# Cluster numbers through DRAM: broadcast by transfers and compared on VectorE, in place of one-hot rows transposed on TensorE

## The chip, the cores and the metric

The kernel runs on one core of one Trainium2 chip. Its five engines each have an instruction stream of their own: TensorE (PE, with its weight loads PEld), VectorE (DVE), ScalarE (ACT), GpSimd (POOL) and SyncE (SP), which here issues nearly all DMAs. They meet only at semaphores. TensorE writes to PSUM, eight banks of 2 KB a partition; the other operands lie in SBUF. The metric is the device time of one execution in microseconds (us), the median of several runs. All times below come from the runs, the profile's page or the trace.

## What is computed

The reference is a clustered attention, followed by a mixing stage that the change does not touch.

```python
q_n = q / (norm(q) + 1e-06); k_n = k / (norm(k) + 1e-06); c_n = centroids / (norm(centroids) + 1e-06)
q_assign = np.argmax(np.einsum('bhsd,hcd->bhsc', q_n, c_n), axis=-1)
k_assign = np.argmax(np.einsum('bhsd,hcd->bhsc', k_n, c_n), axis=-1)
mask = q_assign[:, :, :, None] == k_assign[:, :, None, :]
scores = scale * np.matmul(q, k.transpose(0, 1, 3, 2))
scores = np.where(mask, scores, -1000000000.0)
attn = softmax(scores)              # shifted by the row's largest score
x = np.matmul(attn, v)              # then: theta = x @ w_theta, rotation, token mixing, channel layer
```

There are 4 batches, 8 heads, 768 positions, 64 numbers a head and 16 clusters. Every query and every key belongs to the cluster whose centroid fits it best, and a query sees only the keys of its own cluster.

## The kernel before

**Pairs and units.** Two heads fill the 128 partitions, 64 each, so there are 16 pairs (`pi`, 0 to 15). The attention of a pair is cut into 12 units: for each half of the queries (`a`, 384 positions) the six blocks of 128 keys. Units are numbered through, 12 to a pair, and the loop `while u < NUT + LAG or todo` writes the work of one unit after another. `in_order` (L440) ties the instructions of each engine, SP included, into exactly that order. Work that is not needed in every unit is entered in a list `todo` by `at_unit` and `stages`, and is written at the end of its unit, behind what every unit has.

What a unit holds, in its order:

- `scores(u)` (L335): eight matmuls (four products for each head), then the exponentials on ScalarE (L344) and a running sum on GpSimd (L350). The products are q's and k's high and low parts, and one product of the masks `mk` and `mq`.
- in odd units `row_max(u + 11)` (L304): eight matmuls of the product and the mask for 128 queries of the unit eleven ahead, then two reductions on VectorE (L319), which give the largest score of each query. The matmuls write to two tiles of two banks each, which the next row maxima take again.
- in even units `weighted` (L387) twice: eight matmuls of exponentials and v (`av`).
- the entries of `todo`.

The mask is a matmul as well. `mq` has, for each head, 16 rows with a one in the row of the query's cluster, and `mk` has -2^60 in the rows of all clusters but the key's own. Row 32 of each half of `mq` gets the query's largest score with the sign turned, brought there by `shift_row` (L323): TensorE transposes the maxima (`mt`), ScalarE copies them (`mr`), and two DMAs write them to the row. So the product adds the mask and the shift to the scores.

**The cluster numbers** are made by the generator `assign(pi)` (L217), one stage per `yield`, entered for pair `pi` by `prepare` (L457) at the units of `A_UNITS`, counted from the start of the pair two before:

1. unit -2: two loads of the raw q and k (`raw`).
2. unit 1: logits of q and k against the centroids (`lg`, eight matmuls), copied to SBUF by ScalarE (`lgs`).
3. unit 3: three transposes (`lt`), so that the positions lie on partitions; VectorE finds the largest logit of each (`mx`) and marks where it is reached (`eq`, L246).
4. unit 4: the marks times the numbers 16 to 1 (L250), and the largest of these is the cluster's number (`rr`, L252).
5. unit 6: `ohp` (L254), a one in the place of the number, by comparing it with all 16.
6. units 9 and 11: six transposes each on TensorE (`ot`, L262) turn the ones of q and of k back, and ScalarE copies them to `mq` (L264) and, scaled and shifted, to `mk` (L266).

Pair 0 goes through all of it at the start, before any unit, and pair 1 in the eleven units with negative numbers, which hold row maxima but no scores.

**Around it.** `part_hi` (ScalarE) and `part_lo` (GpSimd) split q and k into high and low parts, at `HI_UNITS` and `LO_UNITS`. `sums(pi)` (L352) adds up the rows of exponentials on TensorE (`sm`), copies them by ScalarE (`se`), writes them to DRAM, reads them in another layout, takes the reciprocal on VectorE (L378), writes that to DRAM and reads it broadcast over 64 partitions (`rb`), at the units of `SUMS` of the next pair. `normalise` multiplies on GpSimd and writes the result to DRAM, at `NORM`. `early_weights` loads and splits the weights of the later stage, a chunk every 13 units; each chunk costs VectorE two operations four units after its start (L128, L130) and two more eight units after it (L133, L135).

**PSUM.** Scores take two banks of the pool `ps`, which has three (`bank`), and each small piece, `lg`, `lt`, `ot`, `mt` and `sm`, takes one. The banks go round in the order of the program, and a bank is written again only when its last reader is done.

Of the kernel before, what the change touches and what calls it, by code (L numbers as in the profile page):

```python
# [9 lines left out]
F32 = mybir.dt.float32  # L10
F32R = mybir.dt.float32r
BF16 = mybir.dt.bfloat16
I32 = mybir.dt.int32
AF = mybir.ActivationFunctionType
ALU = mybir.AluOpType
# [3 lines left out]
BIG = float(2.0 ** 60)  # L19
N_M = 2  # L20
N_AV = 1
LEAD = 11
PW = 256
TAIL = 2
WARM = 2
SUMS = (5, 6, 8, 10, 12)
NORM = (14, 16)
TERMS = 3
EARLY = 3
LAG = 3  # L30
# [11 lines left out]
def kernel(  # L42
# [19 lines left out]
    nc = tc.nc  # L62
    B, H, D, S = qT.shape
    P = 128
    NP = H // 2
    NT = S // P
    C = cent.shape[0] // H
# [5 lines left out]
    cpool = ctx.enter_context(tc.tile_pool(name="cpool", bufs=1))  # L73
    dram = ctx.enter_context(tc.tile_pool(name="dram", bufs=1, space=bass.MemoryType.DRAM))
# [3 lines left out]
    identf = cpool.tile([P, P], F32, name="identf")  # L78
    make_identity(nc, identf)
    identb = cpool.tile([P, P], BF16, name="identb")  # L80
# [13 lines left out]
    mbi = cpool.tile([P, 1], F32, name="mbi")  # L94
    nc.vector.memset(mbi, 0.0)
    for r in (0, 64):
        nc.vector.memset(mbi[r:r + C], -BIG)
        nc.vector.memset(mbi[r + 32:r + 33], 1.0)

    ecol = cpool.tile([P, 32], F32, name="ecol")  # L100
    nc.vector.memset(ecol, 0.0)
# [65 lines left out]
    pe = actx.enter_context(tc.tile_pool(name="pe", bufs=1))  # L167
    NPAIR = B * NP
    tsets = {}
    for x in range(3):  # L170
        x = (NPAIR + x) % 3
# [7 lines left out]
    def bank(name, pool=None):  # L179
        return (pool or ps).tile([P, 512], F32, tag="bank", name=name)  # L180
# [30 lines left out]

    NG = HS // C

    ohp = pe.tile([P, NG, 64], BF16, name="ohp")
    nc.vector.memset(ohp, 0.0)
    wb = wc.unsqueeze(1).broadcast_to([P, NG, C])
    def assign(pi):  # L217

        b, p = divmod(pi, NP)
        raws = []
        for n, src, eng in (("q", qT, nc.sync), ("k", kT, nc.scalar if pi == 0 else nc.sync)):
            raw = pw.tile([P, S], F32, tag="raw", name=f"raw{n}{pi}", bufs=3)
            st.setdefault(pi, dict(tsets[pi % 3]))["raw" + n] = raw
            eng.dma_start(out=raw, in_=src[b, 2 * p:2 * p + 2].rearrange("h d s -> (h d) s"))
            raws.append(raw)
        yield
        lg = bank(f"lg{pi}")[:, 0:HS]
        for g in range(4):  # L230
            a, n = divmod(g, 2)
            nc.tensor.matmul(  # L232
                lg[32 * g:32 * g + 32], lhsT=cb[:, p, :, :],
                rhs=raws[n][:, a * HS:(a + 1) * HS], start=True, stop=True)
        lgs = pe.tile([P, HS], F32, tag="lgs", name=f"lgs{pi}")
        nc.scalar.copy(out=lgs, in_=lg)
        yield
        lt = bank(f"lt{pi}")[:, 0:HS]
        for t in range(HS // P):
            sl = slice(t * P, (t + 1) * P)  # L240
            nc.tensor.transpose(out=lt[:, sl], in_=lgs[:, sl], identity=identf)
        ltv = lt.rearrange("p (g c) -> p g c", c=C)
        mx = pe.tile([P, NG], F32, tag="mxl", name=f"mxl{pi}")
        nc.vector.tensor_reduce(out=mx, in_=ltv, op=ALU.max, axis=AX.X)
        eq = pe.tile([P, NG, C], BF16, tag="eq", name=f"eq{pi}")
        nc.vector.tensor_tensor(  # L246
            out=eq, in0=ltv, in1=mx.unsqueeze(2).broadcast_to([P, NG, C]), op=ALU.is_equal)
        yield

        nc.vector.tensor_tensor(out=eq, in0=eq, in1=wb, op=ALU.mult)  # L250
        rr = pe.tile([P, NG], BF16, tag="rr", name=f"rr{pi}")
        nc.vector.tensor_reduce(out=rr, in_=eq, op=ALU.max, axis=AX.X)  # L252
        yield
        nc.vector.tensor_tensor(  # L254
            out=ohp[:, :, 0:C], in0=wb, in1=rr.unsqueeze(2).broadcast_to([P, NG, C]), op=ALU.is_equal)
        ohv = ohp.rearrange("p (x n j) c -> p x n (j c)", n=2, j=2)
        for n, x in enumerate(("mq", "mk")):
            yield
            ot = bank(f"ot{pi}{n}").bitcast(BF16)[:, 0:S]
            for t in range(NT):  # L260
                a, y = divmod(t, NH)
                nc.tensor.transpose(out=ot[:, t * P:(t + 1) * P], in_=ohv[:, 2 * y + a, n], identity=identb)  # L262
            if n == 0:
                nc.scalar.copy(out=st[pi][x], in_=ot)  # L264
            else:
                nc.scalar.activation(out=st[pi][x], in_=ot, func=AF.Identity, scale=BIG, bias=mbi)  # L266


    st = {}
# [19 lines left out]
    NH = NT // 2  # L289
# [111 lines left out]
    def normalise(pi):  # L401
        b, p = divmod(pi, NP)
        s = st.pop(pi)

        (nc.gpsimd if pi < NPAIR - 2 else nc.vector).tensor_tensor(
            out=s["xt"], in0=s["xt"], in1=s["rb"], op=ALU.mult)
        yield
        nc.sync.dma_start(out=xT_d[b][:, p], in_=s["xt"].rearrange("p a s -> p (a s)"))

    def early_weights():  # L410
        for c in range(NCT):
            yield from split_w(*w_th[c], w_theta[c * P:(c + 1) * P], DM, raw_pair, nc.gpsimd, CKE)
        for t in range(EARLY):
            for w, src in ((w_r, wrT), (w_i, wiT)):
                yield from split_w(*w[t], src[t * P:(t + 1) * P], S, raw_pair, nc.gpsimd, CKE)
        for c in range(NCT):
            yield from split_w(*w_c[c], w_ch[c * P:(c + 1) * P], DM, raw_pair, nc.gpsimd, CKE)
# [8 lines left out]
    def at_unit(u, fn, *a):  # L426
        todo.setdefault(u, []).append((fn, a))

    def stages(units, gen):

        for u in units:
            at_unit(u, lambda: next(gen, None))
        at_unit(units[-1] + 1, run, gen)
# [15 lines left out]
                tail[ins.engine] = ins.name  # L449


    A_UNITS = (-2, 1, 3, 4, 6, 9, 11)
    HI_UNITS = dict(q=0, k=2)
    LO_UNITS = dict(q=2, k=4)
    W_UNITS = (4, 8, 11)
    W_EVERY = 13
    def prepare(pi, gen):  # L457
        u = NU * (pi - 2)
        stages([u + k for k in A_UNITS[1 if pi == 1 else 0:]], gen)
        for n in "qk":  # L460
            at_unit(u + HI_UNITS[n], part_hi, pi, n)
            at_unit(u + LO_UNITS[n], part_lo, pi, n, nc.gpsimd)


    start = len(nc.cur_bb.bb.instructions)
    g0, g1 = assign(0), assign(1)
    next(g0)
    next(g1)
# [8 lines left out]
    for pi in range(NPAIR):  # L477
        u = NU * pi
        if pi > 0:
            prepare(pi, g1 if pi == 1 else assign(pi))  # L480
            at_unit(u - NU + 7, load_v, pi)
        for a in range(2):
            at_unit(u + a * NT - LEAD + NT, shift_row, pi, a)
        stages([u + NU + k for k in SUMS], sums(pi))
        stages([u + NU + k for k in NORM], normalise(pi))
    for x, gen in enumerate(early_weights()):
        u = W_EVERY * x
# [4 lines left out]
    u = -LEAD  # L492
# [225 lines left out]
    u = None  # L718
    for part in range(S // PW):
# [4 lines left out]
        u = add_y(B - 1, part * PW, (part + 1) * PW)  # L724
# [53 lines left out]
```

## Time and profile before

| | us |
|---|---|
| median of 3 runs | 863.45 |
| lowest and highest run | 861.3 and 863.47 |
| the profiled execution | 864.6 |
| its span on the core | 862.8 |
| granted clock of TensorE, mean | 0.982 of full speed |

| part of the span | us | TensorE busy |
|---|---|---|
| start, to the first row sums | 0 to 79 | partly, at a lower clock at first |
| pairs 1 to 14, from row sums to row sums | 80.67 to 458.64 | 369.11 of 377.97 |
| last pairs and the change to the mixing stage | 459 to 557 | with gaps |
| mixing stage | 557 to 863 | nearly all |

Over the span TensorE is busy 824.7 us, VectorE 466.8, ScalarE 402.5 and GpSimd 470.6. The rows of the profile that carry the argument are in the prediction. In rows of the chain of waits stand start, length, engine, tile and line; in rows of groups the mean of one instruction in ns stands behind the bar; in rows of the timeline the idle time ahead of an instruction and what ended it stand in brackets.

### The profile page before, as it was taken

Reading aid. Unit: us, or ns where it says so; the run is one execution under the profiler, and the core shown is the slowest. Engines: PE = TensorE matmul, PEld = TensorE weight load, DVE = VectorE, ACT = ScalarE, POOL = GpSimd, SP = SyncE. Lnnn points to the kernel's source line nnn. Section 1 sums busy time; section 2 is a strip of 40 time slices with the busy share of each in tenths; the row PEclk is TensorE's granted clock in tenths of the full one; section 3 lists DMA queues with packets and bytes.
Section 4 is the critical chain, followed back from the end, with each engine's and each line's share of the span. In section 5 each row is a group of like instructions: output and inputs, shape, how many; then the busy total and the mean of one; then the engine's idle time right before and its main releaser. Section 6 shows DMA issues by size and latency. Waiting matters only on the chain.

```text
span 862.8 us, 14648 instructions
## 1 busy us (share of the span) xinstructions
PE 824.7 (96%) x5863; PEld 599.2 (69%) x5863; DVE 466.8 (54%) x642; ACT 402.5 (47%) x802; POOL 470.6 (55%) x295
## 2 busy tenths in 40 slices
PE   5899899999999999999999989799999999999998
PEld 2655566565656555555666458589888988899998
DVE  4576576665775686477665188744423442343222
ACT  3246555565656555545655556432333333333220
POOL 3067668767887687677776636735122512251231
PEclk9699999999999999999999999899999999999999
DMA  2211222323223322213331152201200120010001
GB/s 94 65 53 45 88 86 65 128 87 101 80 88 111 112 76 93 81 53 102 99 119 57 56 178 98 73 1 50 98 2 1 50 98 1 1 49 26 1 13 63
DMA packets 27190, 59.09 MB, mean 68 GB/s; under 512 B 7793, under 2 KB 12657, under 8 KB 26737
## 3 DMA queue, kind: packets, MB, share of 16 engines
q1 hardware_dynamic: 26976, 57.75, 21.0%
q8 instruction: 46, 0.75, 0.4%
q10 hardware_dynamic: 144, 0.39, 0.1%
q14 instruction: 24, 0.19, 0.1%
HBM read 45.25 MB, written 12.78 MB: 67 GB/s over the span
## 4 chain that ended last, share of the span: by engine, by line
PE 77%; DVE 14%; DMA 4%; issue 2%; ACT 2%; POOL 1%; SPq 0%; ACTq 0%; DVEq 0%; POOLq 0%
PE y L648 21%; PE sc L300 16%; PE av L393 12%; PE m L300 7%; PE tp L581 6%; PE cy L671 4%; DVE nm L319 4%; PE cp L671 2%; DMA rawq<-in_qT_dram 2%; PE lg L232 2%; PE sm L360 2%; PE ot L262 1%; DVE w L130 1%; DVE w L135 1%; DVE eq L250 1%
## 5 line engine op out<-in xcount | busy, mean ns | idle before, releaser
L319 DVE TENSOR_REDUCE nm<-m 128x1 f32<-128x768 f32 x192 | 174.6, 950 | 145.5 <-PE m L300 145.5
L344 ACT ACTIVATE at<-sc 128x384 f32<-128x384 f32 x384 | 167.3, 489 | 122.8 <-PE sc L300 118.1
L350 POOL TENSOR_TENSOR acc<-at,at 128x768 f32<-128x768 f32 x64 | 120.7, 1886 | 99.7 <-ACT at L344 99.6
L393 PE MATMUL av<-at,vt 128*64 128x384 f32 x768 | 145.8, 501 | 0.0
L350 POOL TENSOR_TENSOR acc<-acc,at 128x768 f32<-128x768 f32 x64 | 123.1, 1923 | 28.9 <-ACT at L344 27.7
L602 POOL TENSOR_TENSOR zlc<-ab,zhc 128x512 fp32r<-128x512 f32 x24 | 31.9, 1330 | 170.8 <-ACT zhc L600 169.5
L300 PEld LDWEIGHTS sc<-hq,hk 64*128 64x128 f32 x384 | 41.4, 185 | 88.1 <-ACT at L344 60.9
L300 PE MATMUL sc<-hq,hk 64*128 64x384 f32 x384 | 92.4, 442 | 2.4 <-ACT at L344 2.4
L393 PEld LDWEIGHTS av<-at,vt 128*64 128x64 f32 x768 | 46.9, 137 | 59.4 <-issue 54.7
L300 PE MATMUL m<-hk,hq 64*128 64x384 f32 x384 | 76.1, 355 | 9.1 <-DVE nm L319 9.0
L300 PE MATMUL m<-mk,mq 64*128 64x384 f32 x384 | 73.5, 352 | 0.4 <-ACT mk L266 0.4
L300 PE MATMUL sc<-lq,hk 64*128 64x384 f32 x384 | 71.7, 340 | 0.0
L300 PE MATMUL sc<-mq,mk 64*128 64x384 f32 x384 | 70.8, 338 | 0.0
L300 PE MATMUL sc<-hq,lk 64*128 64x384 f32 x384 | 70.7, 338 | 0.0
L585 DVE TENSOR_SCALAR kk<-tp 128x512 int32<-128x512 f32 x24 | 16.5, 689 | 98.9 <-PE tp L581 98.9
L662 POOL TENSOR_TENSOR ul<-xT,uh 128x384 fp32r<-128x384 f32 (+1 forms) x36 | 33.9, 965 | 42.5 <-ACT uh L661 35.8
L576 ACT COPY xn<-xp 128x512 f32<-128x512 f32 x24 | 14.0, 585 | 88.6 <-PE xp L574 88.6
L648 PE MATMUL y<-wr_hi,zhc 128*128 128x512 f32 (+1 forms) x216 | 52.9, 320 | 1.8 <-ACT zhc L600 1.8
L300 PEld LDWEIGHTS m<-hk,hq 64*128 64x128 f32 x384 | 43.0, 193 | 15.4 <-DVE nm L319 15.0
L648 PE MATMUL y<-wr_hi,zlc 128*128 128x512 f32 (+1 forms) x216 | 52.9, 321 | 0.0
L648 PE MATMUL y<-wr_lo,zhc 128*128 128x512 f32 (+1 forms) x216 | 52.7, 320 | 0.0
L648 PE MATMUL y<-wi_hi,zhs 128*128 128x512 f32 (+1 forms) x216 | 52.5, 319 | 0.0
(143 smaller groups left out, 1641.0 us busy)
## 6 DMA issues: line engine op xcount, KB each, us to landing
rawq<-in_qT_dram SPq DMA_DIRECT2D x16, 384.0 KB
vt<-in_v_dram SPq DMA_DIRECT2D x16, 384.0 KB
rb<-sd SPq DMA_DIRECT2D x32, 192.0 KB
xT_d<-xt SPq DMA_DIRECT2D x16, 384.0 KB
rawk<-in_kT_dram SPq DMA_DIRECT2D x15, 384.0 KB
xT<-xT_d SPq DMA_DIRECT2D x3, 1536.0 KB
out_dram<-ot SPq DMA_DIRECT2D x24, 192.0 KB
w<-in_wrT_dram SPq DMA_DIRECT2D x3, 768.0 KB
```

Of the source, the lines that this page charges most:

```text
L232: nc.tensor.matmul(lg[32 * g:32 * g + 32], lhsT=cb[:, p, :, :], rhs=raws[n][:, a * HS:(a + 1) * HS], start=True, stop=True)
L300: nc.tensor.matmul(outs[j], lhsT=stat[r, cols], rhs=mov[r, over], start=(n == 0), stop=(n == len(products) - 1))
L319: nc.vector.tensor_reduce(out=s["nm", a][:, j, i // 2:i // 2 + 1], in_=m[j][:, :, 0:HS], op=ALU.max, axis=AX.XY, negate=True)
L344: last_exp[0] = nc.scalar.activation(out=at[:, j], in_=sc[j], func=AF.Exp, scale=SCALE)
L350: last_acc[0] = nc.gpsimd.tensor_tensor(out=s["acc", a, x], in0=prev, in1=at, op=ALU.add)
L360: nc.tensor.matmul(sm[32 * g:32 * g + 32], lhsT=ecol, rhs=s["acc", a, x][:, j], start=(x == 0), stop=(x == NT // TERMS - 1))
L393: nc.tensor.matmul(s["av"][64 * j:64 * j + 64], lhsT=s["vt"][:, i, j, :], rhs=s["at", a, i][:, j], start=(i == 0), stop=(i == NT - 1))
L581: nc.tensor.matmul(tp, lhsT=xx[:, c, :], rhs=w_th[c][k], start=(n == 0), stop=(n == 3 * NCT - 1))
L602: nc.gpsimd.tensor_tensor(out=zl, in0=tr, in1=zh.bitcast(F32), op=ALU.subtract)
L648: nc.tensor.matmul(y_at(b, d, c0, c1), lhsT=zz[:, d * P:(d + 1) * P], rhs=ww[:, c0:c1], start=first and lead, stop=last, skip_group_check= ...
L662: nc.gpsimd.tensor_tensor(out=ul[:, d, :], in0=x, in1=uh[:, d, :].bitcast(F32), op=ALU.subtract)
L671: nc.tensor.matmul(cp, lhsT=w_c[d][k][:, e * P:(e + 1) * P], rhs=uu[:, d, :], start=(n == 0), stop=(n == 3 * NCT - 1), skip_group_check=True)
```

## The change

The one-hot rows and their transposes go. The cluster number of each position (`rr`, now in fp32) is transposed once on TensorE, so that 24 rows of 128 positions lie one below the other (`rt`), copied by ScalarE (`ri`) and written to DRAM (`rd`). Four DMAs read it back, each one head's numbers of q or k broadcast over 16 partitions of a tile `cl`. VectorE compares the tile with the number that each partition stands for (`mcl`) and writes `mq` directly, and `mk` by a compare and a multiplication in one instruction. The rows of `cl` that no transfer writes hold -100, set once by GpSimd. The transposes `lt` write their columns in another order, so that the 24 rows come out in the order of heads and positions.

The units are moved too. The raw loads go two units ahead. Logits, `lt`, `rt`, the row sums and the row shifts, all that TensorE does in small pieces, stand in even units, behind `av`; before, they stood in odd units, behind the row maxima. `sums` and `normalise` move one unit ahead, `shift_row` one unit ahead, `part_hi` one unit back. The stages of `assign` are now: -4 raw loads, 0 logits, 2 `lt` with `mx` and `eq`, 3 `rr`, 4 `rt` and its copy, 5 the write, 7 the four reads, 9 `mq`, 10 `mk`.

```diff
-SUMS = (5, 6, 8, 10, 12)
-NORM = (14, 16)
+SUMS = (4, 5, 7, 9, 11)
+NORM = (13, 15)
...
+    mci = cpool.tile([P, 1], I32, name="mci")
+    for r in (0, 64):
+        nc.gpsimd.iota(mci[r:r + 64], pattern=[[0, 1]], base=C, channel_multiplier=-1)
+    mcl = cpool.tile([P, 1], F32, name="mcl")
+    nc.vector.tensor_copy(out=mcl, in_=mci)
...
-    ohp = pe.tile([P, NG, 64], BF16, name="ohp")
-    nc.vector.memset(ohp, 0.0)
+    cl = {n: pe.tile([P, S], F32, name=f"cl{n}") for n in "qk"}
+    for n in "qk":
+        nc.gpsimd.memset(cl[n], -100.0)
...
+        ltp = lt.rearrange("p (g a t c) -> p a g t c", a=2, t=NH, c=C)
         for t in range(HS // P):
             sl = slice(t * P, (t + 1) * P)
-            nc.tensor.transpose(out=lt[:, sl], in_=lgs[:, sl], identity=identf)
+
+            nc.tensor.transpose(out=ltp[:, :, :, t], in_=lgs[:, sl], identity=identf)
...
-        rr = pe.tile([P, NG], BF16, tag="rr", name=f"rr{pi}")
+        rr = pe.tile([P, NG], F32, tag="rr", name=f"rr{pi}")
         nc.vector.tensor_reduce(out=rr, in_=eq, op=ALU.max, axis=AX.X)
         yield
-        nc.vector.tensor_tensor(
-            out=ohp[:, :, 0:C], in0=wb, in1=rr.unsqueeze(2).broadcast_to([P, NG, C]), op=ALU.is_equal)
-        ohv = ohp.rearrange("p (x n j) c -> p x n (j c)", n=2, j=2)
-        for n, x in enumerate(("mq", "mk")):
-            yield
-            ot = bank(f"ot{pi}{n}").bitcast(BF16)[:, 0:S]
-            for t in range(NT):
-                a, y = divmod(t, NH)
-                nc.tensor.transpose(out=ot[:, t * P:(t + 1) * P], in_=ohv[:, 2 * y + a, n], identity=identb)
-            if n == 0:
-                nc.scalar.copy(out=st[pi][x], in_=ot)
-            else:
-                nc.scalar.activation(out=st[pi][x], in_=ot, func=AF.Identity, scale=BIG, bias=mbi)
+
+        rt = bank(f"rt{pi}")[0:NG, 0:P]
+        nc.tensor.transpose(out=rt, in_=rr, identity=identf)
+        ri = pe.tile([NG, P], F32, tag="ri", name=f"ri{pi}")
+        nc.scalar.copy(out=ri, in_=rt)
+        yield
+        rd = dram.tile([NG, P], F32, tag="rd", name=f"rd{pi}", bufs=2)
+        nc.sync.dma_start(out=rd, in_=ri)
+        yield
+        rv = rd.rearrange("(g t) x -> g (t x)", t=NT)
+        for n, x in enumerate("qk"):
+            for j in range(2):
+                nc.sync.dma_start(
+                    out=cl[x][64 * j:64 * j + C], in_=rv[2 * n + j:2 * n + j + 1].broadcast_to([C, S]))
+        yield
+        nc.vector.tensor_scalar(out=st[pi]["mq"], in0=cl["q"], scalar1=mcl, scalar2=None, op0=ALU.is_equal)
+        yield
+        nc.vector.tensor_scalar(
+            out=st[pi]["mk"], in0=cl["k"], scalar1=mcl, scalar2=mbi, op0=ALU.not_equal, op1=ALU.mult)
...
-    A_UNITS = (-2, 1, 3, 4, 6, 9, 11)
-    HI_UNITS = dict(q=0, k=2)
+    A_UNITS = (-4, 0, 2, 3, 4, 5, 7, 9, 10)
+    HI_UNITS = dict(q=1, k=3)
     LO_UNITS = dict(q=2, k=4)
...
-            at_unit(u + a * NT - LEAD + NT, shift_row, pi, a)
+            at_unit(u + a * NT - LEAD + NT - 1, shift_row, pi, a)
```

## The prediction

> **What bounds the kernel now.** I read the page first, then the chain of waits over the attention stage, then the windows cut at successive row sums, then single instructions. The change touches only that stage, the first 490 us. A "pair" below is two heads, 12 units of work.
>
> ```profile
> span 862.8 us, 14648 instructions
> 80.67:458.64 377.97, 369.11 (x3020) 221.05 (x3022) 248.65 (x279) 220.81 (x464) 286.12 (x155) 1.00 0.30 93
> 80.67:110.93 30.26, 27.96 (x235) 16.86 (x237) 18.49 (x23) 16.87 (x36) 20.26 (x13) 1.00 0.27 84
> 110.93:138.82 27.89, 27.89 (x235) 16.88 (x237) 18.97 (x23) 17.05 (x36) 21.22 (x13) 1.00 0.30 92
> 138.82:167.42 28.60, 28.33 (x235) 16.98 (x237) 19.06 (x23) 17.01 (x36) 21.31 (x12) 1.00 0.30 89
> ```
>
> Columns of the last four: stretch, length, busy time of PE, PEld, DVE, ACT, POOL, granted clock, DMA share and GB/s. A window from one row sum to the next is one pair. In 110.93:138.82 TensorE is busy for all of its 27.89 us: a clean pair is bound by TensorE's own order. Thirteen pairs took 377.97 us where thirteen clean ones take 362.6, so 15.4 us are stalls.
>
> The chain of waits shows of what a clean pair is made. First an odd and the following even unit with a one-hot piece (ot) whole; then the lengths of the other pieces, row shift (mt), logits (lg), transposed logits (lt) and row sums (sm); last, near the end of the stage, two starts between which no piece stands:
>
> ```profile
> 290.44 0.91 PE sc L300 x7
> 291.35 0.70 PE m L300 x8
> 292.05 0.44 PE ot L262 x6
> 292.49 0.90 PE sc L300 x8
> 293.39 1.44 PE av L393 x8
> 294.84 0.89 PE sc L300 x5
> ...
> 300.84 0.20 PE mt L327
> 301.05 0.78 PE lg L232 x8
> ...
> 246.12 0.48 PE lt L241 x3
> ...
> 457.14 1.43 PE sm L360 x16
> ...
> 465.25 0.89 PE sc L300 x8
> ...
> 469.18 0.90 PE sc L300 x8
> ```
>
> Bare: 465.25 to 469.18, 3.93 us. With ot: 290.44 to 294.84, 4.40 us. Every odd unit of a pair carries one such piece now: shift and logits (unit 1), lt (3), sm (5), shift (7), ot (9 and 11). Six bare double units are 23.6 us; the pieces and their switches make the other 4.3.
>
> Of the 15.4 us of stalls, two kinds stand on the chain:
>
> ```profile
> 93.62 0.15 DVE sq L378
> ...
> 94.21 4.13 DMA rawq<-in_qT_dram
> ...
> 149.40 5.41 DMA rawq<-in_qT_dram
> ...
> 207.61 4.29 DMA rawq<-in_qT_dram
> ...
> 353.09 6.45 DMA rawq<-in_qT_dram
> ...
> 310.06 1.93 DVE w L133
> ...
> 314.49 1.74 DVE nm L319 x2
> ...
> 316.28 0.97 PE m L300 x7
> ```
>
> First, the load of raw q is issued right behind the write of the reciprocal sums in SP's queue, and that write waits for VectorE's reciprocal (93.62, 94.21); four times the logits then come late. The windows price the first two at 30.26 - 27.9 = 2.4 and 28.60 - 27.9 = 0.7; I put about 1 us on each of the others: 5 in all. Second, VectorE jams: a weight chunk's operations (w), with the cluster numbers' own four ahead of them in the same gap, stand before the row maxima, and PE's next row scores wait (314.49, 316.28). That is the remaining 10.4.
>
> **The change part by part.**
>
> *Pieces.* The 12 ot transposes of a pair go, one transpose of 24 columns (rt) comes, and the pieces sit behind av in even units: shift and logits in 0, lt in 2, sm and rt in 4, a shift in 6. No piece behind av is in the trace. I take them at their own lengths from the chain, since the switch from av to the next scores is already inside the bare 3.93: 0.20 + (0.20 + 0.78) + 0.48 + 1.43 + 0.20 for rt (as mt) = 3.3. A pair is then 26.9 instead of 27.9: -1.0, and for the 14 pairs that prepare another, **-14.0**. Bounds: -1.0 and, if each keeps the price it has in odd units, -0.7. In the last two pairs four shifts lose their 0.2 switch: **-0.8**.
>
> *The bank behind sm.* Three PSUM banks rotate over scores and pieces. Unit 4 now holds two pieces, so the second head of unit 5's scores takes sm's own bank and must wait for ScalarE's copy of it:
>
> ```profile
> 224.07 0.44 PE L300 MATMUL sc<-hq,hk 64*128 64x384 f32 x2
> ...
> 224.21 0.58 ACT L366 ACTIVATE se<-sm,eps 128x384 f32<-128x384 f32 x1 [1.23 <-PE sm L360]
> ```
>
> PE was free of sm at 224.07, the copy ended at 224.79, 0.72 later; rt and the switch fill 0.26: 0.46 a pair, **+6.4**. Bounds 0 (the heads overlap the wait) and 0.8 a pair (rt itself waits: rr is ready about when sm ends, with no slack).
>
> *Masks on VectorE.* The one-hot compare (ohp) goes, as do ScalarE's two mask copies, whose time is hidden under the matmuls now. Two compares of 768 elements with per-partition numbers come, behind the maxima of unit 9:
>
> ```profile
> L130 DVE TENSOR_SCALAR w<-w 128x512 int32<-128x512 int32 x8 | 11.0, 1371 | 0.3
> L199 DVE TENSOR_SCALAR cnn<-cin,cs 128x128 f32<-128x128 f32 x1 | 0.3, 286 | 0.0
> L196 DVE TENSOR_SCALAR cs<-cs 128x1 f32<-128x1 f32 x1 | 0.2, 154 | 0.7 <-POOL cs L195 0.7
> L130 DVE TENSOR_SCALAR w<-w x14: 427/561/1947, 50.7 to 460.3; 128x512 int32<-128x512 int32 x8, 128x768 int32<-128x768 int32 x6
> 466.87 0.96 DVE L319 TENSOR_REDUCE nm<-m 128x1 f32<-128x768 f32 x1 [2.49 <-PE m L300]
> L350 POOL TENSOR_TENSOR acc<-at,at 128x768 f32<-128x768 f32 x64 | 120.7, 1886 | 99.7 <-ACT at L344 99.6
> ```
>
> L199 is the nearest row, for it too has a number per partition: (286 - 154) / 127 = 1.04 ns an element, so 0.95 us for 768. L130 with plain constants does 0.54 ns, 0.57 us, but is often held: 0.427 at best, 1.371 on average for 512. Bounds 0.57 and 1.95 each; I take 0.95.
>
> What waits behind them is new. The shift transpose now stands one unit behind its row maxima, not two. In a bare double unit the maxima start 1.69 after the scores (465.18, 466.87) and take 1.8: VectorE is free at 3.5; unit 11's maxima are ready at 3.93 + 1.69 = 5.62 and must have begun by 7.86 - 1.8 = 6.06, when PE reaches mt. Room is 2.55 for the reciprocal (0.22) and both compares (1.9): it fits, with 0.4 to spare. Since they vary, I take 0.2 a pair: **+2.8** (bounds 0 and 1.6 a pair).
>
> The Trainium skill, page "SBUF — State Buffer", section "Who interferes with whom", speaks against this part: a tensor_scalar in a two-port mode takes the port pair shared with GpSimd for a whole instruction and whichever comes second is blocked fully. L130's spread from 0.427 to 1.947 agrees with it. By it the compares would cost as in the rival below if they ran in that mode, and 0.95 each unblocked if they did not.
>
> *Loads of raw q and k* move two units ahead, past the reciprocal's write: the logits come only one unit sooner, so the four waits go: **-5.0** (bounds -5 and 0, if the five new issues of SP, one write and four broadcasts at about 0.4 each, put the loads back; what stands ahead of them waits for DMAs, not for VectorE). The broadcasts are issued two units before the compares, about 4 us against 1.5 of issue and 1.5 of landing: hidden. If not, VectorE waits with the maxima behind it.
>
> *Sums, normalise and the copies of hq and hk* move by one unit with all their transfers; the distances within each chain stay. I cost them at nothing: their cover is GpSimd, idle 92 of the 377.97 us. What shrinks is the lead of hq and hk over lq and lk, two units to one; if these wait, GpSimd's accumulations behind it come late, and sm, now a unit sooner, with them.
>
> *VectorE's jams.* mxl and eq now fall between unit 1's and 3's maxima, eq and rr between 3's and 5's: four operations no longer in one gap. But mt in 0 and 6, and rt, wait on VectorE directly, and 9 to 11 is now full. Chunks of weights come every 13 units, pairs every 12, so each gap meets a chunk once or twice whatever is done. I count about 12 us where 10.4 are now: **+2.0** (bounds -5 and +6).
>
> *The prologue* has no cover; PE waits for pair 0's masks.
>
> ```profile
> 5.00 0.46 PE cps L203
> ...
> 10.94 0.56 DVE rr L252
> ...
> 14.65 1.33 PE m L300 x6
> ...
> 27.55 0.25 ACT L329 CAST mr<-mt 6x128 fp32r<-6x128 f32 x1 [8.48 <-PE mt L327]
> ...
> 484.38 0.54 SPq L373 DMA_DIRECT2D sd<-se  x1
> 486.06 0.32 SPq L376 DMA_DIRECT2D sq<-sd  x1
> 487.59 0.23 DVE L378 RECIPROCAL sq<-sq 128x12 f32<-128x12 f32 x1 [14.24 <-DMA sq<-sd]
> ```
>
> From rr's end (11.50) to the first masked product is 3.15 now. After: rt 0.46 (as cps, cold), copy 0.25 (as mr), write to dependent read 1.68 (484.38 to 486.06), three further issues at 0.38, landing 1.53 (486.06 to 487.59), the last compare 0.95, gaps 0.3: 6.3. That is +3.1; the second ot of pair 1, on the chain just before the first scores, goes, 0.44 when warm and more at the prologue's lower clock: **+2.5** (bounds +1.5 and +6). The two fills of the cluster tiles on GpSimd lie in its idle time ahead of lq, while ScalarE makes hq, and cost nothing there.
>
> Sum: 2.5 - 14.0 + 6.4 + 2.8 - 5.0 + 2.0 - 0.8 = -6.1. The profiled execution took 864.6 us (span 862.8 and 1.8 around it), so it becomes 858.5; the median of the runs, 863.45, becomes **857.4**.
>
> **The rivals.**
>
> *Slower: the compares queue behind GpSimd.* If each is a 0.57 instruction that waits on average half of one of GpSimd's 1.89, it takes 1.5. With the reciprocal that is 3.2 against room for 2.55: unit 11's maxima come 0.67 late and PE stands at mt, 9.4 us over 14 pairs in place of 2.8, and for the four weight chunks that meet this gap about 1 us more each. 863.45 - 6.1 + 6.6 + 4 = 868. It decides from about 1.2 us a compare. For it: L130, held as often as not. Against it: L199's rate, that of an instruction without doubling.
>
> *The new waits stay hidden.* No wait for sm's bank and none at mt: 863.45 - 6.1 - 9.2 = 848. For it: ScalarE and VectorE are idle 42% and 34% of the 377.97 us. Against it: the order in which the bank is freed is fixed.
>
> *The change doesn't do what it says: even units are no cheaper.* Pieces keep the 0.40 (mt) and 0.55 (lt) that they cost beside a bare unit: a saving of 0.7 a pair in place of 1.0, so +4.2: 861.6. For it: nothing in the trace shows a piece behind av.
>
> **How the numbers follow.** Forecast 0.50 (its own range 850 to 863), compares queue 0.18, waits hidden 0.14, pieces no cheaper 0.18. About 0.3%, 2.6 us, is what a measurement here can tell from no change. Faster by more: most of the forecast (0.43), hidden waits (0.14), some of the third rival (0.05): 0.62. Within: 0.20. Slower: nearly all of the first rival and the forecast's edge: 0.18. The range, 846 to 869, takes in all three rivals; beyond it lie jams at their lower bound together with hidden waits, and compares that each wait out a whole GpSimd instruction.
>
> **What would show it.** Right: a clean pair near 27.5 us between row sums; sc behind sm longer than 0.90 on the chain; no raw load on the chain behind the reciprocal; the first masked product near 17.8 us; compares near 0.95 each with little spread. Wrong: compares of 1.5 or more; PE idle at mt or rt, released by VectorE, in most pairs; VectorE idle on the broadcasts; pieces behind av that cost 0.1 or more beyond their length.

## The result, and the profile after

| | before | after |
|---|---|---|
| median | 862.38 us (4 runs, 859.12 to 863.47) | 897.25 us (4 runs, 896.06 to 898.81) |
| ratio after to before, 95% interval | | 1.041 [1.038, 1.045] |
| span of the profiled execution | 862.8 us | 894.3 us |

The change makes the kernel 4.1% slower; 857.4 had been forecast, in a range of 846 to 869. The groups of the first score products (one row for each kernel) give for the smallest, median and largest instruction its ns, then the first and the last start in us. They cut the execution into three parts. First before, then after:

```profile
L300 PE MATMUL sc<-hq,hk x384: 335/439/687, 34.4 to 493.8; 64*128 64x384 f32 x192
```

```profile
L315 PE MATMUL sc<-hq,hk x384: 330/437/687, 40.0 to 525.9; 64*128 64x384 f32 x192
```

| part | before | after | difference | forecast |
|---|---|---|---|---|
| start to the first scores | 34.4 | 40.0 | +5.6 | +2.5 |
| first to last scores, the 192 units | 459.4 | 485.9 | +26.5 | -8.6 |
| last scores to the end | 369.0 | 368.4 | -0.6 | 0 |

(A forecast for the units is the sum of all terms but the prologue's.) The loss is in the units. The windows from row sum to row sum in the kernel after answer to those shown of before; first the thirteen pairs together, then a long one and two clean ones:

```profile
82.57:487.38 404.81, 367.11 (x2877) 231.20 (x2878) 272.24 (x291) 201.25 (x451) 286.55 (x154) 0.95 0.29 93
114.37:147.51 33.14, 29.79 (x222) 18.63 (x221) 20.34 (x23) 15.54 (x35) 20.87 (x13) 0.90 0.25 83
147.51:175.21 27.70, 27.07 (x222) 17.02 (x222) 20.23 (x24) 15.56 (x36) 20.29 (x12) 1.00 0.35 109
175.21:203.06 27.85, 27.32 (x222) 17.03 (x222) 19.03 (x24) 15.88 (x36) 21.36 (x13) 1.00 0.25 81
```

A clean pair came out much as forecast, 27.7 where about 27.5 had been named. But ten of the thirteen pairs take 29.4 to 35.1 us. TensorE is idle for 404.81 - 367.11 = 37.7 us of the thirteen, where it was 377.97 - 369.11 = 8.9 before, and its mean clock falls from 1.00 to 0.95. What it waits for is named by the view of TensorE's waits in the same stretch (line waited at, releaser, us in total, times, longest), first after, then before:

```profile
PE mt L342 <- DVE nm L334: 22.0, 16, 3.2
PE rt L265 <- DVE rr L261: 11.8, 9, 5.2
PE sc L315 <- DVE eq L255: 3.4, 2, 1.9
```

```profile
PE m L300 <- DVE nm L319: 4.6, 9, 1.0
PE lg L232 <- ACT at L344: 3.6, 3, 2.3
```

(At `lg` the view names the semaphore that came last; what came late there in the kernel before are the raw loads that the prediction read on the chain.) In the kernel after nearly all of it is VectorE, at the two places where a small piece stands one unit behind what VectorE makes for it: the transpose of the row maxima (`mt`) and that of the cluster numbers (`rt`). How a wait at `mt` comes about is seen in VectorE's timeline between units 9 and 11 of one pair (start, length, line, operation; in brackets the idle time ahead of it):

```profile
92.83 1.82 DVE L334 TENSOR_REDUCE nm<-m 128x1 f32<-128x768 f32 x2 [2.12 <-PE m L315]
94.57 0.22 DVE L393 RECIPROCAL sq<-sq 128x12 f32<-128x12 f32 x1
94.71 2.12 DVE L278 TENSOR_SCALAR mq<-clq,mcl 128x768 fp32r<-128x768 f32 x1
96.75 0.68 DVE L139 SCALAR_TENSOR_TENSOR w<-w,w 128x512 int32<-128x512 int32 x1
97.46 2.19 DVE L141 SCALAR_TENSOR_TENSOR w<-w,w 128x512 int32<-128x512 int32 x1
99.58 0.67 DVE L280 TENSOR_SCALAR mk<-clk,mcl,mbi 128x768 fp32r<-128x768 f32 x1
100.17 1.81 DVE L334 TENSOR_REDUCE nm<-m 128x1 f32<-128x768 f32 x2
```

And GpSimd beside it:

```profile
94.58 1.83 POOL L365 TENSOR_TENSOR acc<-at,at 128x768 f32<-128x768 f32 x1 [1.66 <-ACT at L359]
97.15 1.96 POOL L365 TENSOR_TENSOR acc<-acc,at 128x768 f32<-128x768 f32 x1 [0.73 <-ACT at L359]
```

From 92.83 to 101.98 VectorE has no gap. The compare `mq` starts 0.13 after GpSimd's accumulation and ends 0.42 after it; the chunk's L141 starts 0.31 after the next one and ends 0.54 after that. So each of these two seems to have sat out most of a GpSimd instruction. Between the end of the first maxima and the start of the last the forecast had 0.22 + 1.9 us of work in a room of 2.55; here it is 5.6, from 94.57 to 100.17, and the 3.05 that are too much are TensorE's wait at `mt`. The chain of waits shows what that wait costs beyond itself (start, length, engine, tile, line, count):

```profile
102.12 0.27 PE mt L342
102.39 1.09 PE lg L239 x8
103.48 1.58 PE sc L315 x8
105.06 1.25 PE m L315 x8
106.31 0.70 PE sc L315 x6
```

The same pieces took 0.78, 0.90 and 0.70 in the chain of before. The windows around it show why; the third number from the end of a row is the granted clock:

```profile
98.00:102.30 4.30, 1.25 (x9) 0.31 (x5) 3.98 (x4) 0.46 (x2) 1.11 (x1) 1.00 0.24 93
102.30:104.00 1.70, 1.70 (x13) 0.75 (x14) 0.00 (x0) 0.73 (x3) 0.00 (x0) 0.63 0.00 0
104.00:106.00 2.00, 2.00 (x16) 2.00 (x14) 0.00 (x0) 1.37 (x5) 1.28 (x1) 0.50 0.24 43
106.00:108.00 2.00, 2.00 (x20) 1.17 (x16) 1.66 (x2) 1.62 (x4) 1.90 (x2) 0.96 0.56 221
```

TensorE stood for 3 us and then ran at half its clock for about as long. At `rt` the same happens with the chunk's operations ahead of the numbers; the chain there:

```profile
264.59 2.55 DVE w L139
...
267.16 2.46 DVE w L141
269.62 1.73 DVE nm L334 x2
271.36 1.91 DVE eq L259
...
273.29 0.56 DVE rr L261
...
273.99 0.37 PE rt L265
274.36 1.58 PE sc L315 x6
```

Two operations of a weight chunk, 5 us between them, stand ahead of the maxima and the numbers, and TensorE waits 5.2 us for a transpose of 0.37.

### The profile page after: what moved, and what is told of

Same layout as the page of the kernel before. It is cut to its first block, busy times and chain, and to the rows that moved or that the text cites. A ratio compares the mean times of both kernels' runs of the same rounds, so it can differ in the third digit from the quotient of the medians.

```text
span 894.3 us, 14486 instructions
## 1 busy us (share of the span) xinstructions
PE 817.8 (91%) x5687; PEld 605.8 (68%) x5687; DVE 493.9 (55%) x658; ACT 378.8 (42%) x786; POOL 472.3 (53%) x299
## 4 chain that ended last, share of the span: by engine, by line
PE 65%; DVE 23%; DMA 4%; issue 3%; ACT 2%; SPq 2%; POOL 1%; DVEq 0%; ACTq 0%; POOLq 0%
PE y L663 20%; PE sc L315 12%; DVE nm L334 8%; PE av L408 7%; PE tp L596 6%; PE m L315 6%; PE cy L686 4%; PE cp L686 2%; PE lg L239 2%; DVE mq L278 2%; DVE eq L259 2%; DVE w L134 1%; DVE w L141 1%; DVE w L139 1%; DVE mk L280 1%
## 5 line engine op out<-in xcount | busy, mean ns | idle before, releaser
L315 PE MATMUL sc<-hq,hk 64*128 64x384 f32 x384 | 101.6, 426 | 6.2 <-DVE eq L255 3.4
L315 PEld LDWEIGHTS sc<-hq,hk 64*128 64x128 f32 x384 | 55.3, 192 | 58.2 <-ACT at L359 25.9
L315 PE MATMUL sc<-lq,hk 64*128 64x384 f32 x384 | 88.2, 358 | 0.0
L315 PE MATMUL sc<-hq,lk 64*128 64x384 f32 x384 | 84.0, 348 | 0.0
L315 PE MATMUL sc<-mq,mk 64*128 64x384 f32 x384 | 83.9, 347 | 0.0
L315 PE MATMUL m<-hk,hq 64*128 64x384 f32 x384 | 73.9, 361 | 1.1 <-DVE nm L334 1.1
L315 PEld LDWEIGHTS sc<-hq,lk 64*128 64x128 f32 x384 | 54.7, 195 | 0.0
L315 PEld LDWEIGHTS sc<-mq,mk 64*128 64x128 f32 x384 | 54.7, 196 | 0.0
```

The source lines that it names most:

```text
L315: nc.tensor.matmul(outs[j], lhsT=stat[r, cols], rhs=mov[r, over], start=(n == 0), stop=(n == len(products) - 1))
```

## The experiments

Each run goes with runs of the kernel before on the same chip; ratios are to those. All of them compute the whole reference. First one table; the parts are cut as above, from each run's own profile.

| run | what it is | median us | ratio to before | to first scores | 192 units | rest |
|---|---|---|---|---|---|---|
| before | | 862.4 | | 34.4 | 459.4 | 369.0 |
| after | | 897.3 | 1.041 [1.038, 1.045] | 40.0 | 485.9 | 368.4 |
| e1 | before, even units | 868.2 | 1.008 [1.005, 1.011] | 35.1 | 460.3 | 369.9 |
| e2 | before, masks on VectorE | 877.3 | 1.017 [1.012, 1.022] | 37.1 | 469.9 | 369.0 |
| e3 | after, shift one unit later | 871.3 | 1.012 [1.008, 1.016] | 39.0 | 460.4 | 369.8 |
| e4 | e3, numbers earlier | 850.0 | 0.987 [0.983, 0.990] | 39.2 | 440.7 | 368.1 |
| e5 | one-hot masks, e4's units | 854.0 | 0.992 [0.990, 0.995] | 34.7 | 451.3 | 371.1 |
| e6 | after, compares later | 874.1 | 1.016 [1.010, 1.021] | 39.7 | 463.6 | 368.5 |
| e7 | after, other chunk units | 849.5 | 0.986 [0.980, 0.992] | 40.4 | 438.7 | 369.3 |
| e8 | e4, pair 0 by one-hot | 848.9 | 0.986 [0.981, 0.991] | 35.1 | 444.0 | 367.3 |
| e9 | before, other chunk units | 849.2 | 0.985 [0.983, 0.988] | 33.5 | 444.8 | 368.9 |
| e10 | e8, other chunk units | 838.7 | 0.973 [0.970, 0.976] | 34.9 | 432.8 | 368.0 |
| e11 | after, load of v later | 894.3 | 1.040 [1.034, 1.045] | 39.8 | 484.5 | 367.2 |
| e12 | e1, other chunk units | 849.0 | 0.984 [0.981, 0.987] | 35.4 | 443.7 | 368.1 |

(The profiled execution of e5 was its slowest, 858.9; of the others it lies within 2.3 us of the median.)

### Which half of the change: e1 and e2

e1 leaves the masks as before and takes the units of the change (edit to the kernel before):

```diff
-SUMS = (5, 6, 8, 10, 12)
-NORM = (14, 16)
+SUMS = (4, 5, 7, 9, 11)
+NORM = (13, 15)
...
-    A_UNITS = (-2, 1, 3, 4, 6, 9, 11)
-    HI_UNITS = dict(q=0, k=2)
+    A_UNITS = (-4, 0, 2, 3, 5, 8, 10)
+    HI_UNITS = dict(q=1, k=3)
...
-            at_unit(u + a * NT - LEAD + NT, shift_row, pi, a)
+            at_unit(u + a * NT - LEAD + NT - 1, shift_row, pi, a)
```

> The one-hot masks of before with the even units: pieces behind av, row shift one unit behind its maxima, loads of raw q and k two units ahead; ohp in unit 5, its transposes in 8 and 10. Theory W (TensorE now stands directly at mt and rt for VectorE, and each longer wait also lowers its clock): rt is not there and the gap from unit 9 to 11 is light, so the waits at mt are few, 5 us or less in all, against 22 in the changed kernel, and the time lies within 855 to 870. Theory M (the compares and their transfers cost it in whatever unit): this has none of them, so it is faster than before, near 850.

For e2 the masks are made as in the kernel after, and the units are the odd ones of before (edit to the kernel after):

```diff
-SUMS = (4, 5, 7, 9, 11)
-NORM = (13, 15)
+SUMS = (5, 6, 8, 10, 12)
+NORM = (14, 16)
...
-    A_UNITS = (-4, 0, 2, 3, 4, 5, 7, 9, 10)
-    HI_UNITS = dict(q=1, k=3)
+    A_UNITS = (-2, 1, 3, 4, 5, 6, 8, 10, 11)
+    HI_UNITS = dict(q=0, k=2)
...
-            at_unit(u + a * NT - LEAD + NT - 1, shift_row, pi, a)
+            at_unit(u + a * NT - LEAD + NT, shift_row, pi, a)
```

> The compares and transfers of the changed kernel in the old odd units: row shift two units behind its maxima, lt in 3, rr in 4, rt in 5, write 6, reads 8, compares 10 and 11. Theory W: waits at mt fall from 22 us to 5 or less; rt still stands one unit behind rr and still waits, some 10 us; about 875. Theory M: most of the loss is still there, 888 or more, with VectorE's compares between the row maxima on the chain.

Each half alone costs something, 6.3 and 15.4 us against the 861.9 us of the kernel before beside them, together some 22; both at once cost 35. So neither half is the culprit by itself: they make each other dearer. In e1 the shift's transpose is already the place where TensorE waits: 14.1 us for the maxima at `mt` over the whole span, up to 3.1 at a time, where theory W had 5 or less, though its time is in W's range. In e2 it is `rt`, with 10.0 us, as theory W had it.

### Which wait: e3, e4 and e6

e3 undoes one line of the change:

```diff
-            at_unit(u + a * NT - LEAD + NT - 1, shift_row, pi, a)
+            at_unit(u + a * NT - LEAD + NT, shift_row, pi, a)
```

> The changed kernel with the row shift alone two units behind its maxima again, in odd units. Theory W: the 22 us of waits at mt go to 3 or less, and with them the low clock behind them; 872 to 880. Theory M: the wait only moves to the next row scores, 890 or more.

e4 also gives `rr` two units of distance to `rt`:

```diff
-    A_UNITS = (-4, 0, 2, 3, 4, 5, 7, 9, 10)
+    A_UNITS = (-6, -2, 0, 1, 4, 5, 7, 9, 10)
```

> As the run before, and raw loads, logits, lt and rr two units earlier, so that rr stands three units ahead of rt; compares where they are. Theory W: waits at rt, 11.8 us in the changed kernel, go to 2 or less as well; 860 to 868. Theory M: no better than the run before.

e3 takes 25.5 us off the units, and with them the waits at `mt` (26.8 us over the whole span in the kernel after); `rt` is left, 13.3 us over the whole span. e4 takes another 19.7 off and leaves `rt` 2.8 us. Its 850.0 is 10 us below the range of its theory W, e3's 871.3 just below. With one unit of room more at `mt` and two more at `rt` the change is 1.4% faster than before, with the same compares, the same transfers and the same weight chunks.

e6 leaves the shift early and moves the compares out of the gap between 9 and 11:

```diff
-    A_UNITS = (-4, 0, 2, 3, 4, 5, 7, 9, 10)
+    A_UNITS = (-4, 0, 2, 3, 4, 5, 7, 11, 12)
```

> The changed kernel with its two compares moved from units 9 and 10 to 11 and 12, behind the maxima that the row shift of unit 0 waits for. Theory W: the waits of mt in unit 0, about half of the 22 us, go, with the low clock behind them; those in unit 6 and at rt stay; 878 to 885. If the compares cost their time in any gap: 893 or more.

It comes to 874.1, below theory W's 878 to 885: the gap at 9 was crowded by the compares, and 22 us of the units went with them, but over the whole span `mt` still waits 13.0 us and `rt` 18.1, for the chunks still meet the other gaps.

### What collides: e7

A gap is the time that VectorE has between the row maxima of one odd unit and those of the next. The pairs come every 12 units and the chunks every 13, so a chunk's operations wander through a pair. In the thirteen pairs of the kernel after TensorE waits twelve times for more than 1 us, and VectorE's timeline has two operations of a chunk in the unbroken run of work ahead of each of the twelve; no wait without a chunk ahead of it is longer than 0.54 us. e7 lets them stand still, with VectorE's two halves at units that have room:

```diff
-    W_UNITS = (4, 8, 11)
-    W_EVERY = 13
+    W_UNITS = (4, 7, 11)
+    W_EVERY = 12
...
-        u = W_EVERY * x
+        u = W_EVERY * x + 1
```

> The changed kernel with one weight chunk every 12 units in place of 13 and VectorE's two pairs of weight operations always in units 5 and 8, never in the gaps of units 1 to 4 and 9 to 11. Theory J (single waits are 0.2 to 0.5 us; the long ones come only where a weight chunk meets a gap that is full): 866 to 874, no wait at mt or rt above 1 us. If the gaps are too full even without a chunk: 888 or more.

This one edit to the kernel after takes 48 us away, far more than theory J's 23 to 31. The windows of its thirteen pairs, and TensorE's waits in them:

```profile
79.73:441.20 361.47, 354.42 (x2877) 221.17 (x2878) 263.66 (x295) 200.78 (x453) 286.29 (x155) 1.00 0.33 104
```

```profile
PE rt L265 <- ACT se L381: 4.5, 6, 0.8
PE mt L342 <- DVE nm L334: 1.5, 7, 0.2
```

Against the kernel after the same 2877 matmuls are busy 354.42 us in place of 367.11, and the idle time is 7.1 in place of 37.7: of the 43.3 us between them 30.6 were waits, and the 12.7 by which the same matmuls took longer go with the lower clock behind the waits, 0.95 on average where e7 has 1.00. (The split is good to a few us: at the full clock these matmuls are busy 354.42 us here and 356.93 in e10 below, for short waits inside a row seem to count as busy.) The thirteen pairs lie between 26.8 and 28.2 us, and no wait at `mt` or `rt` in them is above 1 us, as theory J had it.

The view's `se` at `rt` needs a second look:

```profile
107.34 0.55 DVE L261 TENSOR_REDUCE rr<-eq 128x24 f32<-128x384 bf16 x1
107.36 0.58 ACT L381 ACTIVATE se<-sm,eps 128x384 f32<-128x384 f32 x1 [2.08 <-PE sm L375]
108.04 0.27 PE L265 MATMUL rt<-identf,rr 128*24 128x128 f32 x1 [0.75 <-ACT se L381]
```

The cluster numbers `rr` and the copy `se` end together, at 107.89 and 107.94. In the other six `rr` is earlier, and `rt` starts before that copy does (191.55 against 191.69). So it is `rr` that `rt` waits for in these six, even with no chunk near.

### The prologue, and the transfers: e8 and e11

e8 is e4 with the masks of pair 0 alone made by one-hot rows on TensorE, as before; pairs 1 to 15 stay on VectorE.

```diff
+        if pi == 0:
+            nc.vector.tensor_tensor(
+                out=ohp[:, :, 0:C], in0=wb, in1=rr.unsqueeze(2).broadcast_to([P, NG, C]), op=ALU.is_equal)
...
+                    nc.tensor.transpose(out=ot[:, t * P:(t + 1) * P], in_=ohv[:, 2 * y + a, n], identity=identb)
...
+            return
```

> The run with row shift back and early rr, and pair 0's masks alone made by one-hot rows and transposes, so that the start has no trip through DRAM. The prologue's price as forecast, 2.5 to 3.5 us less: 846 to 848. If the later start is made up for by then: 850, as that run.

The first scores come 4.1 us sooner than in e4, and 3.3 of these are lost again in the units (444.0 against 440.7). The total, 848.9, lies between the two outcomes and decides for neither. Every operation stands in the same unit as in e4, so no chunk has moved to another gap; three pairs are longer, and in the first of them VectorE's `mk` behind a chunk is on the chain with 2.32 us, where it takes 0.67 in e4. Why an earlier start does that isn't shown.

e11 issues the load of v two units later, so that it stands behind the four broadcasts in SP's queue:

```diff
-            at_unit(u - NU + 7, load_v, pi)
+            at_unit(u - NU + 9, load_v, pi)
```

> The kernel after, with the 384 KB load of v issued two units later (unit 9 in place of 7), behind the broadcasts on their queue. It prices the three late broadcasts (2.9, 5.4 and 2.1 us on the chain). If the load of v is what makes them late: 888 to 893 and no transfer of the clusters on the chain. If they are late by the store of the clusters and its issue alone: 895 to 899, as after, with the transfers still on the chain.

Its 894.3 (892.8 to 901.1) lies between the two outcomes and is not to be told from after's 897.3 (896.1 to 898.8). In the units of the kernel after three broadcasts for q and one for k stand on the chain, in e11 one for q, and that took at most a few us off. In e7, where the chunks alone moved, none stands on the chain of the units. So the late broadcasts explain no more than a few of the 35 us.

### What the change is worth without the collision: e9, e12, e5 and e10

e9 and e12 are the kernel before and e1, each with the edit of e7 alone.

> The kernel before, with the weight chunks alone in the timetable that took 48 us off the kernel after (every 12 units instead of 13, at the stages 4, 7 and 11, one unit later). It prices the chunks without the change. If weight chunks meeting full gaps cost the kernel before about 10 us too (its pairs of 30.3, 31.5, 29.3 and 33.7 us beside some of 27.9), it comes to 850 to 854, and the change is then worth no more than 1 to 5 us once the chunks are out of its way (849.5 was the kernel after with them). If the kernel before has room enough that chunks don't matter to it, it stays at 858 to 862, and the change itself is worth the whole 10 to 12 us.

> The kernel before with the even units alone (the first run of this study: 868.2), and the new timetable of the chunks. It prices the timetable of TensorE's pieces and sums without masks through memory and without collisions. If the tight timetable costs only where a chunk meets a gap: 850 to 854, and then the masks through memory are worth 0 to 4 us beside the 849.5 of both together. If TensorE's wait for the half's maxima costs by itself: 860 or more.

Both come to 849, as e7 does: 849.2, 849.0 and 849.5. The kernel before had been losing 13 us to its chunks all along, and once nobody collides the change is worth nothing as it stands: its units are 6.1 us shorter (438.7 against 444.8), and its prologue 6.9 longer (40.4 against 33.5). Of e12's two outcomes the second, that TensorE's wait for the maxima costs by itself, is out; by the first, masks through memory are worth nothing beside the 849.5 of both together. Half of e12's pairs take 27.6 us, with the twelve transposes of the one-hot rows still in them.

e5 asks the same with the old chunks: one-hot masks, but sums and pieces in the units of e4 (edit to the kernel before, with `SUMS`, `NORM` and `HI_UNITS` as in e1).

```diff
-    A_UNITS = (-2, 1, 3, 4, 6, 9, 11)
+    A_UNITS = (-6, -2, 0, 1, 4, 8, 10)
```

> The one-hot masks of before in the timetable of the run with early rr (even units, row shift two units behind its maxima, raw loads, logits, lt and rr early; ohp in unit 4, its transposes in 8 and 10). Theory T (what that run gained over the kernel before is its timetable, and the masks through DRAM save little): 850 to 854. Theory P (the transposes taken off TensorE make the gain): 858 or more.

It is at 0.992 of before where e4 is at 0.987: in the same timetable, with the old chunks, masks through memory are worth about half a per cent, at the edge of what the two intervals tell apart.

e10 joins what helped: the change, the shift at its old unit, the numbers two units earlier, pair 0 by one-hot, and the chunks every 12 units.

> The fastest version so far (first product of a half at its old unit, maxima and clusters one unit earlier, pair 0's masks by one-hot on TensorE: 848.9) with the new timetable of the chunks. If tight timetable and chunks are two separate costs, its pairs all come to 27.6 to 28.2 and the time to 843 to 847. If the early maxima had already taken away what the chunks cost, the chunks change nothing and it stays at 847 to 851.

838.7, 2.7% faster than before and below the 843 to 847 expected. The first scores stay early (34.9), and the units are 11.2 us shorter than in e8; no run gives e4 alone the new chunks, so how much of this the early start adds isn't shown. Its group of score products, and the windows of its thirteen pairs and of one:

```profile
L333 PE MATMUL sc<-hq,hk x384: 332/437/448, 34.9 to 467.7; 64*128 64x384 f32 x192
```

```profile
71.73:430.25 358.52, 356.93 (x2877) 221.03 (x2878) 257.90 (x295) 201.63 (x452) 283.88 (x155) 1.00 0.33 105
99.42:127.08 27.66, 27.54 (x223) 17.05 (x222) 19.92 (x23) 15.49 (x35) 21.58 (x13) 1.00 0.31 100
```

Twelve of the thirteen pairs take 27.66 to 27.69 us, the thirteenth 26.42, and in that stretch the view of TensorE's waits has no row at all (the short wait behind `sm`, taken up below, does not show in it). The longest of the score products is 448 ns, where it was 687 before and after: no score ran at half the clock.

## Why the prediction was wrong

**The step that failed is "VectorE's jams", mis-sized.** It said "I count about 12 us where 10.4 are now: +2.0", with +6 as its upper bound. The 10.4 was right: e9 takes the chunks out of the way in the kernel before, and its thirteen pairs come to 367.68 us against 377.97, which is 10.3:

```profile
75.43:443.11 367.68, 362.24 (x3020) 219.54 (x3022) 251.43 (x283) 221.01 (x465) 287.38 (x156) 1.00 0.31 95
```

The 12 was not. e7 takes the same chunks out of the way in the kernel after, and they were 43.3 us in the thirteen pairs. Over all 192 units they cost 14.6 before (459.4 - 444.8) and 47.2 after (485.9 - 438.7), so +32.6 where +2.0 was put. The other terms of the units summed to -10.6, and with the chunks out of the way in both kernels they give -6.1 (438.7 - 444.8); -6.1 and +32.6 make the +26.5 measured. The text had the cause in hand ("mt in 0 and 6, and rt, wait on VectorE directly, and 9 to 11 is now full", "each gap meets a chunk once or twice") and still priced a meeting as before; "PE idle at mt or rt, released by VectorE, in most pairs" stood among its signs of being wrong, and is what came. Three things were left out of the price:

- *There was no more room anywhere.* The room at `mt` was worked out as 2.55 us, with 2.1 of it filled. A chunk's two operations, 0.68 and 2.19 in the gap shown, then become a wait of TensorE, whole. Before, one unit more lay between the maxima and their transpose; e3 gives it back and the units shrink by 25.5 us.
- *A compare and a chunk's operation can each sit out one of GpSimd's instructions*, and a full gap holds more of them. In the gap shown, `mq` and L141 each did, by their times.
- *The clock.* Nothing in the prediction prices what TensorE loses after a wait: about 12.7 of the 43.3 us. The trace's clock records have one stretch of 3.4 us at 0.50 in the thirteen pairs before, and eight, 37.6 us in all, after; so the 10.4 held next to nothing of this cost.

The other steps, by the runs:

- *Pieces: right in the single unit.* In e7's chain a double unit with a shift or an `lt` behind `av` costs the bare 3.93 and the piece:

```profile
307.40 0.20 PE mt L342
307.60 0.89 PE sc L315 x7
...
310.11 1.44 PE av L408 x8
311.55 0.90 PE sc L315 x8
...
324.82 0.48 PE lt L250 x3
325.30 0.90 PE sc L315 x8
...
327.79 1.44 PE av L408 x8
329.24 1.47 PE sm L375 x16
```

  From 307.60 to 311.55 are 3.95, from 325.30 to 329.24 are 3.94. The rival "even units are no cheaper" is out. Pieces, bank and `mt` together were to give -1.0 + 0.46 + 0.2 = -0.34 a pair. The three clean pairs of the kernel after take 27.6 to 27.85 where 27.9 was, so -0.3 at best. Of e7's pairs those that prepare another take 27.6 to 27.8, and 28.0 to 28.2 where `rt` waits 0.75 for `rr`, which the bank term had named as its upper bound; their mean is 27.89, no gain at all. That is about the 4.5 us by which the other terms of the units fell short, -6.1 for -10.6.
- *The bank behind `sm`: right.* The chain of e10, where `rr` is ready early, goes through it in every pair:

```profile
127.00 0.06 PE sm L393 x3
...
127.08 0.59 ACT se L399
...
127.72 0.96 PE sc L333 x7
```

  `sm` ends at 127.06 and the next scores start at 127.72: 0.66, of which `rt` and the switch fill 0.26 as forecast, so 0.40 where 0.46 was put.
- *Raw loads: right.* What the kernel before loses in thirteen pairs beyond thirteen clean ones is 15.4 us, and e9 still loses 367.7 - 362.6 = 5.1 of them, with a raw load on the chain of eight pairs and TensorE waiting for the logits:

```profile
PE lg L232 <- ACT at L344: 5.4, 8, 1.1
```

  The forecast's split was 5.0 and 10.4. In e7 no raw load is on the chain of the units; in the kernel after one is (at 315.22), and TensorE does not wait at `lg`.
- *Compares: wrong in rate, with no harm by itself.* 0.95 with little spread was expected. The rows of the kernel after:

```profile
L278 DVE TENSOR_SCALAR mq<-clq,mcl x16: 546/1334/2124, 16.3 to 473.5; 128x768 fp32r<-128x768 f32 x16
L280 DVE TENSOR_SCALAR mk<-clk,mcl,mbi x16: 667/670/2200, 17.3 to 475.2; 128x768 fp32r<-128x768 f32 x16
```

  Free, they take 0.55 and 0.67, about the lower bound of 0.57; `mq` is mostly held, at a median of 1.33. The nearest row was the wrong one: the two short rows gave 1.04 ns an element, and 768 elements took 0.7 and 0.9, all included. The Trainium skill, page "SBUF — State Buffer", section "Who interferes with whom", says that a tensor_scalar in a two-port mode and GpSimd shut each other out for a whole instruction; the trace agrees with it for `mq` (2.12 at most, GpSimd's accumulation 1.9). The rival "compares queue behind GpSimd" had the mechanism and not the place where it decides: in e10 `mq` is held as often (mean 1.30 us), and TensorE has no wait at `mt` or `rt` in its pairs.
- *Prologue: mis-sized, +2.5 against +5.6.* The first masked product was to come near 17.8 and came at 18.07. The rest was not foreseen: the shift's transpose, a unit sooner here too, waits 1.37 us for its maxima (30.95 in TensorE's timeline), and behind it in SP's queue stand the broadcasts of pair 1, the last of which lands at 36.71, on the chain to the first scores. e3, with the shift back, has the first scores 1.0 us sooner; e8 shows what the trip of pair 0 through memory costs them: 4.1 us.
- *Sums, normalise, the copies of hq and hk: right, nothing.* e12 moves them as the change does and comes to 849.0 where e9 has 849.2. The broadcasts, costed at nothing, came late four times in the units, and by e11 this was worth a few us at most.

## What to carry to other kernels

Before an operation is moved closer to the engine that it waits for, add up what else ever stands in that gap, at its longest rather than its mean, and price one meeting as the wait and the slow clock that may follow it; here one unit of margin at `mt` and two at `rt` cost nothing in TensorE's order and were worth 45 us. Work of another period (13 units against 12) is found by the pairs that come out long while others are clean; giving it the same period and a place of its own gained 13 us in the kernel before, more than the change itself. Compare a change against a baseline that has been freed of the same collision, or it is credited or charged with it.

## What the runs showed of the hardware

- *The clock drops after short waits.* Behind the wait of 3.05 us that ends at 102.12 the granted clock is 0.50 until about 106, behind the one of 5.21 that ends at 273.99 until about 280; pieces of 0.78, 0.90 and 0.70 us take 1.09, 1.58 and 1.25. Even one wait of 1.93 us (`mt` at 310.34) was followed by 3.4 us at 0.50, and one of 1.94 (341.72) by none. In the clock records of the thirteen pairs after, five stretches at 0.50 last 3.41 us and three 6.83, and their starts lie whole multiples of 3.41 apart; how much of such a step must be idle stays open. In e7, whose longest wait in the pairs is 0.8, the clock is 1.00 throughout them. The Trainium skill, page "TensorE: Matmul & The Clock Gate", section "Part 1: The HAM clock gate", has two states and a free-running window of about 3.4 us, with the half clock after at least one idle window: the half clock and the lengths agree, but here waits of 1.93 to 3.18 us sufficed, and not every time.
- *`mk` behind `mq` is rarely held.* Its median is 0.670 with a minimum of 0.667, three of the sixteen took 1.6 to 2.2, and in e7 all sixteen lie between 0.668 and 0.679, though GpSimd is busy for 286.29 of those 361.47 us: the second of two such instructions mostly found the way free.
